# A fused attention and mixer kernel: the second-pass flag made behind the last output products, one output product in halves, 20 instead of 16 products of zeros at the begin, one transposition later

## The chip, the cores and the metric

The kernel runs on 1 core of one Trainium2 chip. A core has a matrix engine (TensorE, PE in the profile, with its weight loads as a row of their own, PEld), three engines for work on vectors (VectorE, DVE; ScalarE, ACT; GpSimd, POOL), and SyncE (SP), which here only issues DMAs. Each engine takes its instructions in the order in which they were written and waits on semaphores for the others. A "q" behind a name (SPq, ACTq, PEldq) means the instruction queue of that engine: DMA issues, loads of a register and branches. The metric is the device time of one execution in microseconds (us); less is better.

## The reference

With x of 2048 tokens by 448 features, float32 throughout:

```
g = sigmoid((x * gate_w).sum(-1))
a = attention(x): 16 heads of 28, one shared k and v (x @ wk, x @ wv),
    softmax(q k^T / sqrt(28)) v, heads joined, @ wo
h  = gelu(layernorm(x) @ w1); each quarter of h shifted by +1, -1, +2, -2 tokens
x1 = x + shifted(h) @ w2
b  = x1 + gelu(layernorm(x1) @ w3) @ w4
out = g * a + (1 - g) * b
```

## The kernel before, in words

The operands of the projections are split into a high part (type `fp32r`) and the rest, and summed from three products, which is why one projection of 512 columns is eleven matmuls (`proj`, lines 134 to 140). The order of the instructions on each engine is the order of the program; no planner moves them.

**The begin.** Line 66 writes a tile of zeros (`warm`), and lines 96 to 98 multiply it 16 times with itself into a bank that nobody reads. PE then waits for the first chunk of `wqraw` (query weights, loaded by ACT's queue, line 292) and of `xkv` (the transposed input, SP's queue, line 293). `first_queries` (line 317 on) begins with eight matmul instructions straight on these float32 chunks (line 324) and goes on with 32 on the split chunks (line 328), which ACT (`wqh`, `ahk`) and DVE (`wql`, `alk`) make meanwhile. After it come `stage_q(4)` to `stage_q(11)`, each eleven matmuls into one bank, a copy by ACT (`qf`, line 316) and a DMA to memory (`qd`, line 317).

Between these stages stands the preparation of the mixer. `centre_w1` (lines 397 to 402) takes the mean out of `w1raw`: PE makes `wsum_ps` in the one bank called "misc", DVE reads it four times (line 401). `ln1_tile` takes the layernorm statistics of a token tile on DVE, and POOL makes 1/sigma of them (`rs_s`, line 149). `ln1_send(0)` transposes that on PE into the same bank "misc" (`rsT`, line 377), ACT copies it out (`rT`, line 379), SP stores it (`rsd`, line 381); `ln1_read(0)` reads it back spread over 112 partitions (`rsb`, line 386). SP issues in order, so the loads of the last quarter of x (`load_x(3)`, line 281; `load_x1(3)`, line 284) stand behind that read. `split_w_high` and `split_w_low` make `w1h` and `w1l` on ACT and DVE. `stage_w1(0)` needs `w1h`, `w1l`, and for its first DVE step (`hf`, line 453) `rsb`. `spare_h` and `spare_w2` move rows by DMA (lines 413 to 416 and 430 to 433) ahead of the products `hs` of `stage_w2` (line 471 on).

**The middle.** `stage_w1`, `stage_w2`, the MLP with w3 and w4, and then attention: 16 units (4 token blocks by 4 groups of 4 heads), 8 rounds each of scores (line 205), exponentials on ACT (line 872), values (line 883). The diff doesn't touch them.

**The end.** The last unit's sums over keys are made by lines 986 to 996: DVE puts the last parts together as `oo` (two halves of 256 tokens), PE adds up the denominators (`sums_to_queries`, line 1002), DVE takes reciprocals (`rr`, line 1009), PE spreads them over rows (line 1012), DVE multiplies (`on`, line 1016). Then `tail_wo` makes the last output products with `wo` (`wo_products`, line 831), adds on DVE (`ot`, line 847) and stores (line 1025). The group before the last (`u - 1`) still owes its product for token tile 3; line 994 puts it into bank 3, and `tail_wo(3, ...)` adds the last group's on top. `check` and the reduction into `worst` (line 1019) say whether any softmax denominator left its range; PE counts the good rows (`n_good`, line 1030), ACT turns the count into an integer (`redo`, line 1032), and every engine loads it (line 1036) and branches (line 1040) past a second pass that these inputs don't need.

Of the kernel before, what the change touches and what calls it, by code (L numbers as in the profile page):

```python
# [17 lines left out]
P = 128  # L18
# [19 lines left out]
def f32(ap):  # L38
    return ap.bitcast(F32)
# [3 lines left out]
def gated_mix_kernel(  # L43
# [12 lines left out]
    nc = tc.nc  # L56
# [33 lines left out]
    def misc_tile(name):  # L90
        return psA.tile([P, 512], F32, tag="misc", bufs=1, name=name)
# [2 lines left out]
        return psA.tile([P, 512], F32, tag="mx", bufs=1, name=name)  # L94

    wps = misc_tile("warm_ps")
    for _ in range(16):
        nc.tensor.matmul(wps[:, 0:256], warm[:, 0:P], warm, start=True, stop=True)

    def split_w_chunk(raw, wh, wl, c, cols=slice(None)):  # L100
# [9 lines left out]
    def split_w_high(raw, wh, wl):  # L110
        nc.scalar.copy(wh[:, 0:3, :], raw[:, 0:3, :])
        nc.gpsimd.memset(f32(wh)[64:128, 3, :], 0.0)
        nc.scalar.copy(wh[0:64, 3, :], raw[0:64, 3, :])
        nc.scalar.copy(wl[64:128, 3, :], raw[64:128, 3, :])

    def split_w_low(raw, wh, wl):
        for c in range(3):
            nc.vector.tensor_tensor(wl[:, c, :], raw[:, c, :], f32(wh)[:, c, :], ALU.subtract)
        nc.vector.tensor_tensor(wl[0:64, 3, :], raw[0:64, 3, :], f32(wh)[0:64, 3, :], ALU.subtract)
# [14 lines left out]
    def proj(ps, wh, wl, ah, al):  # L134
        for c in range(3):
            nc.tensor.matmul(ps, wh[:, c, :], ah[:, c, :], start=(c == 0), stop=False)  # L136
            nc.tensor.matmul(ps, wh[:, c, :], al[:, c, :], start=False, stop=False)  # L137
            nc.tensor.matmul(ps, wl[:, c, :], ah[:, c, :], start=False, stop=False)  # L138
        nc.tensor.matmul(ps, wh[:, 3, :], ah[:, 3, :], start=False, stop=False)  # L139
        nc.tensor.matmul(ps, wl[:, 3, :], ah[:, 3, :], start=False, stop=True)  # L140

    def stats_tile(pool, b, t, mv):
        st = pool.tile([P, 6], F32, tag="st", bufs=4, name=f"st_{pool.name}_{b}_{t}")
        nc.vector.bn_stats(st, x1[:, 4 * b + t, :])
        nc.vector.bn_aggr(mv[:, t, :], st)
# [5 lines left out]
    def stats_tiles(pool, b):  # L151
        return (pool.tile([P, 4, 2], F32, tag="mv", bufs=2, name=f"mv_{pool.name}_{b}"),
                pool.tile([P, 4], F32, tag="rs", bufs=2, name=f"rs_{pool.name}_{b}"))
# [106 lines left out]
    with tc.tile_pool(name="s1b", bufs=1) as s1b, \  # L260
# [34 lines left out]
        w1h = s1.tile([P, 4, D], F32R, name="w1h")  # L295
        w1l = s1.tile([P, 4, D], F32R, name="w1l")
# [16 lines left out]
        def q_out(u, ps):  # L313
            b, g = divmod(u, NG)
            qf = s1.tile([P, 512], F32, tag="qf", bufs=4, name=f"qf_{u}")
            nc.scalar.copy(qf, ps)
            nc.scalar.dma_start(qd[g, :, 512 * b:512 * b + 512], qf)
# [13 lines left out]
        def stage_q(u, tile_of=mm1):  # L331
            b, g = divmod(u, NG)
            ps = tile_of(f"q_{u}")
            w = slice(g * P, (g + 1) * P)
            proj(ps, wqh[:, :, w], wql[:, :, w], *xact[b])
            q_out(u, ps)
# [31 lines left out]
        def ln1_tile(b, t):  # L368
            if t == 0:
                rs1_of[b] = stats_tiles(s1, b)  # L370
            stats_tile(s1, b, t, rs1_of[b][0])
            if t == 3:
                stats_end(*rs1_of[b])

        def ln1_send(b):
            ps = misc_tile(f"rsT_{b}")[0:4, 0:P]
            nc.tensor.transpose(ps, rs1_of.pop(b)[1], ident)
            rT = s1.tile([4, P], F32, tag="rT", bufs=2, name=f"rT_{b}")
            nc.scalar.copy(rT, ps)
            rb_of[b] = dram.tile([4, P], F32, tag="rsd", bufs=2, name=f"rsd_{b}")  # L380
            nc.sync.dma_start(rb_of[b], rT)
# [99 lines left out]
        w1raw = f32(s1b.tile([P, 4, 516], F32R, tag="hl", bufs=2, name="w1raw"))[:, :, 0:D]  # L481
# [28 lines left out]
        centre_w1()  # L510
        stage_q(7)
        stage_q(8)
        ln1_send(0)
        ln1_read(0)
        split_w_high(w1raw, w1h, w1l)
        for t in range(4):
            ln1_tile(1, t)
        split_w_low(w1raw, w1h, w1l)
        stage_q(9)
        load_x(3)  # L520
        stage_q(10)
        load_x1(3)
# [233 lines left out]
    with tc.tile_pool(name="s3", bufs=1, reuse_waits="tile") as s3, \  # L756
# [77 lines left out]
        ot_of = {}  # L834
        whole = slice(0, D)
        halves = [slice(0, D // 2), slice(D // 2, D)]

        def wo_products(u, t, ps, cols=whole, start=True, stop=True):
            by_columns(ps, on_of[u], t, wof[:, u % NG, cols], start, stop)
# [73 lines left out]
        for c in range(NC):  # L913
            u, i = divmod(c, NT // 2)
# [62 lines left out]
        u = NU - 1  # L977
# [6 lines left out]
        wo_banks = [singles[0], singles[1], singles[2], singles[3], pairs[0][:, 1]]  # L984

        for k in (2 * NC - 2, 2 * NC - 1):
            for i in range(2):
                for j in range(4):
                    nc.tensor.matmul(pv[i][32 * j:32 * j + 32, :], vext[:, k % NT, :], p_of[k][:, j, sides[i]],
                                     start=(k % 2 == 0), stop=(k % 2 == 1), tile_position=(0, 32 * j))  # L990
            if k % 2 == 0:
                run_jobs(singles[1], 1)
        assert [job[2] for job in jobs] == [(u - 1, 3), (u - 1, 3)]
        wo_products(u - 1, 3, wo_banks[3][:, whole], stop=False)
        for i in range(2):
            nc.vector.tensor_add(o[:, sides[i]], part[:, sides[i]], pv[i])
        sums = [singles[1][:, 0:8], pairs[1][:, 0, 0:8]]
# [10 lines left out]
        for i in range(2):  # L1008
            nc.vector.reciprocal(rr[:, 8 * i:8 * i + 8], sums[i])
            for t in (2 * i, 2 * i + 1):  # L1010
                for j in range(4):
                    nc.tensor.matmul(rows[i][32 * j:32 * j + 32, t % 2 * P:t % 2 * P + P],
                                     rr[:, 4 * t + j:4 * t + j + 1].broadcast_to([P, 32]), ident,
                                     start=True, stop=True, tile_position=(0, 32 * j))
        for i in range(2):
            nc.vector.tensor_mul(on[:, sides[i]], o[:, sides[i]], rows[i])
        check(rr.rearrange("p (a b) -> p a b", b=4), 4)
# [1 line left out]
        nc.vector.tensor_reduce(worst, good, axis=AX.XY, op=ALU.min)  # L1019
        n0 = NT - 4  # L1020

        def tail_wo(t, ps, cols, queue, start=True):
            wo_products(u, t, ps, cols, start=start)
            wo_add(u, t, ps, cols)
            queue.dma_start(out[0, (n0 + t) * P:(n0 + t + 1) * P, cols], ot_of[n0 + t][:, cols])

        tail_wo(0, wo_banks[0][:, whole], whole, nc.sync)
        tail_wo(1, wo_banks[1][:, whole], whole, nc.scalar)
        n_good = pairs[1][0:1, 0, 0:1]
        nc.tensor.matmul(n_good, worst, ones, start=True, stop=True)  # L1030
        redo = s3.tile([1, 1], mybir.dt.int32, name="redo")
        nc.scalar.activation(redo, n_good, AF.Copy, bias=float(P), scale=-1.0)
        tail_wo(3, wo_banks[3][:, whole], whole, nc.sync, start=False)
        tail_wo(2, wo_banks[2][:, halves[0]], halves[0], nc.scalar)
        tail_wo(2, wo_banks[4][:, halves[1]], halves[1], nc.scalar)
        again = nc.values_load(redo, min_val=0, max_val=P,
                               skip_runtime_bounds_check_because="it is P less a count of at most P flags of 0 or 1")

# [1 line left out]
        with tc.If(again > 0, label="redo"):  # L1040
            for b in range(NB):
                for g in range(NG):
                    u = b * NG + g
# [6 lines left out]
                    for kt in range(NT):  # L1050
                        ps = [bank(f"s2_{u}_{kt}_{j}") for j in range(4)]
# [4 lines left out]
                        for j in range(4):  # L1056
                            nc.tensor.matmul(pv[32 * j:32 * j + 32, :], vext[:, kt, :], p[:, j],
                                             start=(kt == 0), stop=(kt == NT - 1), tile_position=(0, 32 * j))
# [3 lines left out]
                    for t in range(4):  # L1062
                        ps = bank(f"wo2_{u}_{t}")[:, whole]
# [55 lines left out]
```

## Time and profile before

| what | us |
|---|---|
| median of 3 runs (lowest, highest) | 928.12 (927.07, 928.72) |
| the profiled execution, its own time | 929.3 |
| its span, first to last instruction | 927.4 |
| PE busy, share of the span | 913.3 (98%) |
| ACT busy | 636.0 (69%) |
| DVE busy | 519.3 (56%) |

In the rows that follow, a row of the timeline is start, duration, engine, line, operation, output<-inputs, form, count, and in brackets the idle time ahead of it and what ended it. A row of the chain of waits is start, duration, engine, tile and line: the chain runs from the last instruction back, at each step to what released it, and so says which work sets the end. The groups merge instructions that follow each other closely, so that their pieces overlap in print. PEclk in a table of stretches is the share of TensorE's clock that was granted; the record of it begins with the first change of the clock, and what lies ahead of that is printed as 1.00.

### The profile page before, as it was taken

The numbers are of one execution on the slowest core, as the hardware profiler recorded it, in microseconds if no ns is written. First come the engines' busy times: TensorE is split into PE (matmuls) and PEld (weight loads), VectorE is DVE, ScalarE is ACT, GpSimd is POOL, SyncE is SP. The second block draws the span as 40 slices with busy tenths as digits, with TensorE's granted clock in tenths as the row PEclk, the third lists the DMA queues.
The fourth block names the chain that finished last, engine by engine and source line by source line (L and its number), as shares of the span: only waits on it lengthen the run. The fifth ranks groups of instructions, "written<-read, shape, count | busy, mean of one in ns | idle before, by whom it ended". The sixth has DMA issues, their size and how long they took to land.

```text
span 927.4 us, 24251 instructions
## 1 busy us (share of the span) xinstructions
PE 913.3 (98%) x10348; PEld 627.8 (68%) x10348; DVE 519.3 (56%) x965; ACT 636.0 (69%) x1002; POOL 80.3 (9%) x116
## 2 busy tenths in 40 slices
PE   9999999999999999999999999999999999999997
PEld 6788888888888888875555555555555555555553
DVE  3665273631431431146666776777667767766664
ACT  5542345322222132169999999999999999999994
POOL 3243320200000520020000000000000000000000
PEclk9999999999999999999999999999999999999999
DMA  9822643120110110010000001000011000010001
GB/s 309 296 66 55 183 131 126 39 66 1 40 46 2 33 53 1 1 51 23 17 22 21 16 20 49 23 25 15 25 33 39 20 24 14 25 44 13 14 14 43
DMA packets 40584, 47.32 MB, mean 51 GB/s; under 512 B 10137, under 2 KB 28633, under 8 KB 40473
## 3 DMA queue, kind: packets, MB, share of 16 engines
q1 hardware_dynamic: 37160, 40.04, 14.7%
q10 hardware_dynamic: 3312, 5.70, 1.7%
q8 instruction: 82, 1.34, 0.6%
q14 instruction: 30, 0.24, 0.1%
HBM read 32.56 MB, written 11.67 MB: 48 GB/s over the span
## 4 chain that ended last, share of the span: by engine, by line
PE 94%; ACT 4%; issue 1%; DVE 1%; DMA 1%; DVEq 0%; ACTq 0%
PE bank L883 25%; PE bank L205 18%; PE bank L831 5%; PE acc L693 5%; PE acc L695 5%; PE acc L694 5%; PE g L137 4%; PE g L138 4%; PE g L136 4%; ACT p L872 4%; PE pair L205 2%; PE hs L471 1%; PE hs L472 1%; PE g L140 1%; PE g L139 1%; PE h L136 1%
## 5 line engine op out<-in xcount | busy, mean ns | idle before, releaser
L872 ACT ACTIVATE p<-bank 128x512 f32<-128x512 f32 x512 | 265.5, 611 | 11.1 <-POOL ones L857 4.2
L883 PE MATMUL bank<-p,vext 128*32 128x256 f32 x4064 | 248.4, 382 | 5.7 <-ACT p L872 2.0
L883 PEld LDWEIGHTS bank<-p,vext 128*32 128x32 f32 x4064 | 119.0, 109 | 124.4 <-ACT p L872 59.8
L929 DVE COPY p<-pair 128x1024 f32<-128x1024 f32 x127 | 155.6, 1225 | 54.9 <-PE pair L205 40.1
L683 ACT ACTIVATE gh<-g 128x512 fp32r<-128x512 f32 x55 | 32.9, 599 | 187.3 <-PE g L140 187.3
L805 DVE TENSOR_TENSOR o<-o,bank 128x256 f32<-128x256 f32 x222 | 93.5, 421 | 90.1 <-PE bank L883 73.9
L872 ACT ACTIVATE p<-p 128x1024 f32<-128x1024 f32 x127 | 139.8, 1101 | 0.0
L872 ACT ACTIVATE p<-pair 128x1024 f32<-128x1024 f32 x129 | 137.3, 1064 | 0.0
L685 DVE TENSOR_TENSOR gl<-gf,gh 128x512 fp32r<-128x512 f32 x55 | 38.2, 694 | 168.6 <-ACT gf L684 168.6
L205 PE MATMUL bank<-qh,kh 32*128 32x512 f32 x512 | 116.4, 448 | 0.1
L205 PE MATMUL pair<-qh,kh 32*128 32x512 f32 x512 | 116.1, 449 | 0.3 <-DVE x L750 0.3
L205 PE MATMUL bank<-qh,kl 32*128 32x512 f32 x512 | 102.1, 390 | 0.0
L205 PE MATMUL pair<-qh,kl 32*128 32x512 f32 x512 | 101.5, 390 | 0.0
L205 PE MATMUL bank<-ql,kh 32*128 32x512 f32 x512 | 101.3, 388 | 0.0
L205 PE MATMUL pair<-ql,kh 32*128 32x512 f32 x512 | 100.7, 388 | 0.0
L205 PEld LDWEIGHTS bank<-qh,kh 32*128 32x128 f32 x512 | 48.1, 181 | 60.7 <-issue 34.3
L693 PE MATMUL acc<-w4h,gh 128*128 128x448 f32 x220 | 80.6, 366 | 0.0
L695 PE MATMUL acc<-w4h,gl 128*128 128x448 f32 x220 | 80.4, 366 | 0.0
L694 PE MATMUL acc<-w4l,gh 128*128 128x448 f32 x220 | 80.2, 364 | 0.0
L137 PE MATMUL g<-al,w3h 128*128 128x512 f32 x168 | 65.9, 393 | 0.0
L138 PE MATMUL g<-ah,w3l 128*128 128x512 f32 x168 | 65.9, 392 | 0.0
L136 PE MATMUL g<-ah,w3h 128*128 128x512 f32 x168 | 65.8, 392 | 0.0
(210 smaller groups left out, 1402.1 us busy)
## 6 DMA issues: line engine op xcount, KB each, us to landing
qd<-qf ACTq DMA_DIRECT2D x16, 256.0 KB
rb<-rd SPq DMA_DIRECT2D x15, 256.0 KB
x<-in_x_dram SPq DMA_DIRECT2D x4, 896.0 KB
xd<-xt SPq DMA_DIRECT2D x16, 224.0 KB
w34raw<-in_w_dram SPq DMA_DIRECT2D x7, 512.0 KB
qr<-qd SPq DMA_DIRECT2D x64, 56.0 KB
w34raw<-in_w_dram SPq DMA_DIRECT2D x7, 448.0 KB
out_dram<-ot SPq DMA_DIRECT2D x14, 224.0 KB
```

The costliest lines, as they stand in the source:

```text
L136: nc.tensor.matmul(ps, wh[:, c, :], ah[:, c, :], start=(c == 0), stop=False)
L137: nc.tensor.matmul(ps, wh[:, c, :], al[:, c, :], start=False, stop=False)
L138: nc.tensor.matmul(ps, wl[:, c, :], ah[:, c, :], start=False, stop=False)
L205: nc.tensor.matmul(ps[j], k[h, keys], q[h, :], start=(r == 0), stop=(r == 2), tile_position=(32 * j, 0))
L693: nc.tensor.matmul(ps, gh[:, tok], w4h[i][:, k, :], start=(f == 0), stop=False)
L694: nc.tensor.matmul(ps, gh[:, tok], w4l[i][:, k, :], start=False, stop=False)
L695: nc.tensor.matmul(ps, gl[:, tok], w4h[i][:, k, :], start=False, stop=(f == stop))
L805: nc.vector.tensor_add(o, o, pv)
L831: nc.tensor.matmul(ps[32 * i:32 * i + 32, :], a[:, c:c + 32], w, start=start, stop=stop, tile_position=(0, 32 * i))
L872: nc.scalar.activation(p[:, heads], p[:, heads] if source is None else source, AF.Exp, scale=SCALE)
L883: nc.tensor.matmul(pv[32 * j:32 * j + 32, :], vext[:, kt, :], p_of[k][:, j, qs], start=(k == ks[0]), stop=(k == ks[-1]), tile_position=(0, ...
L929: nc.vector.tensor_copy(pa[:, both], pairs[0])
```

## The change

Four edits. The begin has 20 products of zeros in place of 16. The transposition of the first block's 1/sigma, with the copy, the store and the read that follow from it (`ln1_send(0)`, `ln1_read(0)`), stands behind `stage_q(9)` and behind the splits of `w1`; with it `split_w_low` moves ahead of `ln1_tile(1, t)`. At the end the product that the group `u - 1` owes is made in two halves of 224 columns, the second one behind the spreading of the reciprocals. And the flag (`n_good`, `redo`) is made behind the last output product, with the two half stores of tile 2 issued by ACT behind it.

```
     wps = misc_tile("warm_ps")
-    for _ in range(16):
+    for _ in range(20):
         nc.tensor.matmul(wps[:, 0:256], warm[:, 0:P], warm, start=True, stop=True)
...
         stage_q(8)
+        split_w_high(w1raw, w1h, w1l)
+        split_w_low(w1raw, w1h, w1l)
+        for t in range(4):
+            ln1_tile(1, t)
+        stage_q(9)
         ln1_send(0)
         ln1_read(0)
-        split_w_high(w1raw, w1h, w1l)
-        for t in range(4):
-            ln1_tile(1, t)
-        split_w_low(w1raw, w1h, w1l)
-        stage_q(9)
         load_x(3)
...
-        wo_products(u - 1, 3, wo_banks[3][:, whole], stop=False)
+        wo_products(u - 1, 3, wo_banks[3][:, halves[0]], halves[0], stop=False)
...
+        wo_products(u - 1, 3, wo_banks[3][:, halves[1]], halves[1], start=False, stop=False)
         for i in range(2):
             nc.vector.tensor_mul(on[:, sides[i]], o[:, sides[i]], rows[i])
...
-        def tail_wo(t, ps, cols, queue, start=True):
+        def tail_store(t, cols, queue):
+            queue.dma_start(out[0, (n0 + t) * P:(n0 + t + 1) * P, cols], ot_of[n0 + t][:, cols])
+
+        def tail_wo(t, ps, cols, start=True):
             wo_products(u, t, ps, cols, start=start)
             wo_add(u, t, ps, cols)
-            queue.dma_start(out[0, (n0 + t) * P:(n0 + t + 1) * P, cols], ot_of[n0 + t][:, cols])
-
-        tail_wo(0, wo_banks[0][:, whole], whole, nc.sync)
-        tail_wo(1, wo_banks[1][:, whole], whole, nc.scalar)
+        tail_wo(0, wo_banks[0][:, whole], whole)
+        tail_store(0, whole, nc.sync)
+        tail_wo(1, wo_banks[1][:, whole], whole)
+        tail_store(1, whole, nc.scalar)
+        tail_wo(3, wo_banks[3][:, whole], whole, start=False)
+        tail_store(3, whole, nc.sync)
+        tail_wo(2, wo_banks[2][:, halves[0]], halves[0])
+        tail_wo(2, wo_banks[4][:, halves[1]], halves[1])
         n_good = pairs[1][0:1, 0, 0:1]
         nc.tensor.matmul(n_good, worst, ones, start=True, stop=True)
         redo = s3.tile([1, 1], mybir.dt.int32, name="redo")
         nc.scalar.activation(redo, n_good, AF.Copy, bias=float(P), scale=-1.0)
-        tail_wo(3, wo_banks[3][:, whole], whole, nc.sync, start=False)
-        tail_wo(2, wo_banks[2][:, halves[0]], halves[0], nc.scalar)
-        tail_wo(2, wo_banks[4][:, halves[1]], halves[1], nc.scalar)
+        for cols in halves:
+            tail_store(2, cols, nc.scalar)
```

The first place is ACT's row at the begin, where the copy `rT` of the transposed 1/sigma stands among the copies `qf` of the query stages (`qd` is their DMA) and the high parts `w1h` of the weights. Before:

```order
L316 COPY qf_332<-q_320 128x512
L317 DMA qd<-qf_332 128x512
L379 COPY rT_337<-rsT_335 4x128
L111 CAST w1h<-w1raw 128x1344
L113 CAST w1h<-w1raw 64x448
L114 CAST w1l<-w1raw 64x448
L316 COPY qf_379<-q_367 128x512
```

Now:

```order
L316 COPY qf_336<-q_324 128x512
L317 DMA qd<-qf_336 128x512
L111 CAST w1h<-w1raw 128x1344
L113 CAST w1h<-w1raw 64x448
L114 CAST w1l<-w1raw 64x448
L316 COPY qf_375<-q_363 128x512
L317 DMA qd<-qf_375 128x512
L379 COPY rT_380<-rsT_378 4x128
```

`rT` moved behind the three casts and behind the copy and the DMA of the ninth query stage; on PE the transposition `rsT` moved in the same way behind the eleven matmuls of that stage, and the rows of SP and POOL kept their order.

The second place is PE's row at the end, from the denominators (`oo` with `pick`) to the load of the flag; `on_11206` and `on_11210` are the last group's rows, `on_10944` those of the group before it, and `worst` is what the flag is counted from. Before:

```order
L1002 MATMUL pair_3240<-pick,oo_11205 128x4 x2
L1012 MATMUL bank_3237<-ident,rr_11234 32x128 x8
L1012 MATMUL pair_3240<-ident,rr_11234 32x128 x8
L831 MATMUL bank_3235<-wof,on_11206 32x448 x4
L831 MATMUL bank_3236<-wof,on_11206 32x448 x4
L1030 MATMUL pair_3240<-ones,worst 1x1
L831 MATMUL bank_3238<-wof,on_11206 32x448 x4
L831 MATMUL bank_3237<-wof,on_11206 32x224 x4
L831 MATMUL pair_3239<-wof,on_11206 32x224 x4
L1036 TENSOR_LOAD redo
```

Now:

```order
L1002 MATMUL pair_3244<-pick,oo_11209 128x4 x2
L1012 MATMUL bank_3241<-ident,rr_11238 32x128 x8
L1012 MATMUL pair_3244<-ident,rr_11238 32x128 x8
L831 MATMUL bank_3242<-wof,on_10944 32x224 x4
L831 MATMUL bank_3239<-wof,on_11210 32x448 x4
L831 MATMUL bank_3240<-wof,on_11210 32x448 x4
L831 MATMUL bank_3242<-wof,on_11210 32x448 x4
L831 MATMUL bank_3241<-wof,on_11210 32x224 x4
L831 MATMUL pair_3243<-wof,on_11210 32x224 x4
L1039 MATMUL pair_3244<-ones,worst 1x1
L1044 TENSOR_LOAD redo
```

A half of the owed product now stands between the spreading of the reciprocals and the last group's products, and the count of the flag moved from behind the second of these to the very end.

## The prediction

> **What bounds the kernel now.** First the page: who carries the chain of waits.
>
> ```profile
> span 927.4 us, 24251 instructions
> PE 94%; ACT 4%; issue 1%; DVE 1%; DMA 1%; DVEq 0%; ACTq 0%
> ```
>
> TensorE sets the end. The list of what PE waited for over the whole span is short; these come first, and the two rows behind them name DVE:
>
> ```profile
> PE bank L883 <- ACT p L872: 2.0, 7, 0.3
> PE warm_ps L98 <- DVE warm L66: 1.0, 1, 1.0
> PE q L324 <- DMA wqraw<-in_wq_dram: 0.8, 1, 0.8
> ```
>
> The only transfer among them is the first load. After it PE never waits for one, so time taken out of PE's begin should move everything behind it, unless something that is hidden today comes late.
>
> Next the begin: the timeline of PE and of its weight loads, and one row of the chain of waits.
>
> ```profile
> 1.05 3.59 PE L98 MATMUL warm_ps<-warm 128*128 128x256 bf16 x16 [1.05 <-DVE warm L66]
> 5.42 5.86 PE L324 MATMUL q<-xkv,wqraw 128*128 128x512 f32 x8 [0.77 <-DMA wqraw<-in_wq_dram]
> 8.99 0.33 PEld L324 LDWEIGHTS q<-xkv,wqraw 128*128 128x128 f32 x1 [0.52 <-issue]
> 9.83 0.19 PEld L324 LDWEIGHTS q<-xkv,wqraw 128*128 128x128 f32 x1 [0.50 <-issue]
> 10.26 0.19 PEld L324 LDWEIGHTS q<-xkv,wqraw 128*128 128x128 f32 x1 [0.24 <-issue]
> ```
>
> ```profile
> 11.28 7.27 PE q L328 x32
> ```
>
> The same weight load takes 0.33 us at 8.99 and 0.19 from 9.83 on, and the loads follow each other after 0.84 us (9.83 less 8.99), then after 0.43 (10.26 less 9.83). So TensorE's clock doubles at about 9.8. The 3.59 us of zeros did not raise it, and PE then stood idle for 0.77 us; real products raised it 4.4 us after 5.42. From L328 on a product takes 7.27/32 = 0.23.
>
> Last the end of the chain:
>
> ```profile
> 914.09 0.38 PE bank L831 x8
> 915.33 0.75 PE bank L831 x8
> 917.71 0.43 DVE on L1016
> 918.19 2.56 PE bank L831 x19
> ```
>
> At 915.33 the owed product (448 columns, 0.75) stands on the path ahead of the denominators; at 914.09 one of 224 columns takes 0.38.
>
> **The change part by part.** *20 products of zeros.* One takes 3.59/16 = 0.224 us, so 20 end at 1.05 + 4.49 = 5.54, and the hole of 0.77 us closes. Their own price lies between 0 (the hole takes them) and 5.54 - 5.42 = 0.12; I take 0.1. Their worth depends on when the clock rises. If it takes unbroken work, then more than the 3.59 us that weren't enough and at most the 4.4 that were: counted from 1.05 it rises by 5.45, when the first real product starts. The eight L324 products then run at 0.43 throughout. The slow stretch was 9.83 - 5.42 = 4.41 us, half of it lost: 2.2 us. Bounds: 2.2, and 0 if work on zeros doesn't count. I take 2.2, because the row of the 16 zeros is only 0.8 us short of the real products' 4.4; less 0.1, the begin gives 2.1.
>
> What follows must be ready 2.1 us sooner. L328 now starts when L324 ends, 11.28; DVE has its first chunk long before, and the last chunk of weights, for `stage_q(4)`, is ready at 12.26, 6 us ahead of that stage (11.28 + 7.27 = 18.55):
>
> ```profile
> 6.97 0.69 DVE L130 TENSOR_TENSOR alk<-xkv,ahk 128x512 fp32r<-128x512 f32 x1 [5.98 <-ACT ahk L127]
> 11.57 0.69 DVE L103 TENSOR_TENSOR wql<-wqraw,wqh 128x512 fp32r<-128x512 f32 x1 [0.40 <-ACT wqh L102]
> ```
>
> So the 2.1 us pass through.
>
> [...]
>
> *The transposition later.* Left where it is, it would meet these rows:
>
> ```profile
> 29.07 2.21 DVE L401 SCALAR_TENSOR_TENSOR w1raw<-wsum_ps,w1raw 128x448 f32<-128x448 f32 x4
> 31.65 0.27 PE L377 MATMUL rsT<-ident,rs_s 128*4 128x128 f32 x1
> 33.47 0.34 SPq L381 DMA_DIRECT2D rsd<-rT  x1
> 35.16 0.57 ACT L114 CAST w1l<-w1raw 64x448 fp32r<-64x448 f32 x1
> 35.34 0.33 SPq L386 DMA_DIRECT2D rsb<-rsd  x1
> 35.77 0.55 SPq L281 DMA_DIRECT2D xkv<-in_xT_dram  x1
> 42.01 0.69 DVE L453 TENSOR_TENSOR hf<-h,rsb 112x512 f32<-112x512 f32 x1 [0.32 <-PE h L140]
> 52.41 0.69 DVE L453 TENSOR_TENSOR hf<-h,rsb 112x512 f32<-112x512 f32 x1 [0.41 <-DMA rsb<-rsd]
> ```
>
> `rsT` needs the bank that DVE reads until 31.28. At 31.65 it just fits; 2.1 sooner it would hold PE for up to 1.7 us. Behind `stage_q(9)`, eleven products of 0.23 = 2.5 us, it comes at 32.0 and waits for nobody, even if DVE has moved by nothing. What it pushes: `rT` now stands behind the three casts, which end at 35.73, and behind a `qf`; `rsd` is issued near 36.5, the read `rsb` 1.87 later (as 35.34 less 33.47), near 38.4, and `load_x(3)` and `load_x1(3)`, queued behind it on SP, near 38.8: 3 us later. The read that was issued at 35.34 was there for DVE at 42.01, 6.7 us on; DVE now wants it at 39.9, 1.5 us after its issue. So `hf` may come some us late against PE. DVE then has one `hf` (0.69) and one split of that size per group of eleven products (2.5), so it gains 1.1 us a group, and the banks of `h` turn over in fours: PE would feel it after four groups. `w1l` now stands ahead of the statistics on DVE and is ready no later. Counted at nothing; without that cover it is the third rival. POOL's queue is unchanged.
>
> *The half product.*
>
> ```profile
> 914.98 0.42 DVE L996 TENSOR_TENSOR oo<-o,pair 128x256 f32<-128x256 f32 x1
> 917.46 0.62 PE L1012 MATMUL pair<-ident,rr 128*32 128x128 f32 x16
> 920.88 0.57 PE L831 MATMUL pair<-wof,on 128*32 128x224 f32 x8
> ```
>
> It takes 0.75 - 0.38 = 0.37 us from ahead of the denominators; `oo`'s first half is there at 915.40, so they start 0.37 earlier, and so does `on`: ready at 917.77, not 918.14. The other 0.38 follow PE's spreading products, whose last row then ends at 918.08 - 0.37 = 917.71. The timeline prints 0.57 for eight products of 224 columns where the chain has 0.38, so some 0.19 of a row's end is overlapped by what follows: the half runs from about 917.52 to 917.90, and the last group's products start some 0.04 behind it, at 917.94, and not at 918.19. Gain 0.25, between 0.1 (nothing overlaps) and 0.37.
>
> *The flag.*
>
> ```profile
> 919.72 0.17 PE L1030 MATMUL pair<-ones,worst 128*1 128x1 f32 x1
> 921.08 0.16 ACT L1032 ACTIVATE redo<-pair 1x1 int32<-1x1 f32 x1 [6.92 <-PE bank L831]
> 921.85 0.85 ACTq L1025 DMA_DIRECT2D out_dram<-ot  x2
> L1040 SPq EVENT_SEMAPHORE  x8: 17/17/17, 923.0 to 926.0; - x8
> ```
>
> `n_good` leaves the middle of the last products; it overlaps those around it: 0.03 gained, between 0 and 0.17. `redo` must now wait for the last product, 921.45 - 0.28 = 921.17, then 0.17 and 0.16 for itself: 921.5. The half stores queued behind it on ACT wait for DVE's `ot` until 921.85 - 0.28 = 921.57 anyway, so they lose nothing, by 0.07 us; a later flag costs what it is later. The other engines load the flag some 0.2 us later than now, and ACT, whose load stands behind its stores, still branches last. Sum at the end: 0.28.
>
> Together 2.1 + 0 + 0.28 = 2.4 us: the span 927.4 becomes 925.0, the execution's own 929.3 becomes 926.9. The median of the runs shown lies 1.2 us below that profiled execution; 928.12 - 2.4 = 925.7.
>
> **The rivals.** [...]
>
> *Zeros don't count.* No row shows zeros raising the clock. Then the end alone gains: 928.12 - 0.28 = 927.8.
>
> *Slower: the loads pushed back on SP.* `load_x(3)` and the next `rsd` and `rsb` (the DVE row at 52.41 already waited 0.41 for it) run into each other, and the rows that `stage_w2` needs come late:
>
> ```profile
> 54.43 0.59 SPq L433 DMA_DIRECT2D hl<-hl  x1
> 59.74 0.36 PE L471 MATMUL hs<-w2h,hh 128*128 128x448 f32 x1
> ```
>
> Issued at 54.43 and landed, by the 1.87 of `rsd`, at about 56.3, they have 3.4 us now and 1.3 with PE 2.1 us sooner. Past 57.6 PE waits; past 60.0 the whole gain is gone, past 61.9 the kernel is slower by 0.2%: 930.0. That takes a slip of 5.6 us, from loads that start 3 us later. A smaller slip that gives back half of the begin ends at 926.8.
>
> *The last store's tail goes.* SP waits 2.1 us in one piece near the end, while hardly anything moves:
>
> ```profile
> SPq L1040 <- SPq L1040: 3.2, 4, 2.1
> 924.00:924.50 0.50, 0.00 (x0) 0.00 (x0) 0.00 (x0) 0.00 (x0) 0.00 (x0) 1.00 0.00 0
> 925.00:925.50 0.50, 0.00 (x0) 0.00 (x0) 0.00 (x0) 0.00 (x0) 0.00 (x0) 0.50 0.06 9
> q8 instruction: 1, 0.02, 3.2%
> ```
>
> No bytes at 924.0, a trickle until 925.5: some packets of the last store come 1.5 us after the rest. The last row, of the stretch 923.5 to 926, is one code fetch: 3.2% of 16 engines x 2.5 us = 1.3 us of one DMA engine, time enough to hold them up. With the stores 0.28 sooner and PE's branch 0.2 later the fetch may miss them: 925.7 - 1.5 = 924.2, if the timed runs have that tail at all.
>
> **How the numbers follow.** Chances: forecast (925.7) 0.32, fixed stretches (926.1) 0.2, the tail gone too (924.2) 0.2, zeros don't count (927.8) 0.13, half given back (926.8) 0.1, slower (930.0) 0.05. The range goes from 924.2 to 927.8 with 0.2 on each side, since the middle of three runs that spread over 1.65 is no firmer: 924.0 to 928.0. About 0.2% (1.9 us, so 926.3) is what a measurement can tell from no change. Faster: most of the first (0.28), six tenths of the second (0.12) and all of the third, 0.6; slower 0.06; the rest 0.34. The likeliest alone: 925.2 to 926.3.
>
> **What would show it.** Right: no idle PE ahead of L324, weight loads of 0.19 there by 6.4 or earlier, L328 2 us sooner, no transfer among PE's waits behind the first load, `on` 0.37 and the last `ot` 0.28 sooner as counted from the end of the values. Wrong: weight loads of 0.33 up to 9; PE waiting at L377, for a bank of `h` or at L471; the last two stores more than 0.1 us behind their `ot`; SP's last wait longer than 2.1.

## The result, and the profile after

| what | before | after |
|---|---|---|
| median (lowest to highest), 10 runs each, us | 928.63 (927.07 to 931.87) | 925.5 (924.77 to 926.98) |
| ratio, 95% interval | | 0.9964 (0.9954 to 0.9974) |
| the profiled execution, its own time and span, us | 929.3, 927.4 | 925.3, 923.5 |

By the ratio the change makes the kernel 3.3 us faster (2.4 to 4.3); the medians lie 3.1 apart; 925.7 was forecast. The two profiled executions differ by more, 4.0 us of span. The page of the changed kernel, its shares of the chain of waits, and then what PE waited for in the whole span:

```profile
span 923.5 us, 24276 instructions
PE 95%; ACT 3%; issue 1%; DVE 1%; DMA 0%; ACTq 0%
```

```profile
PE bank L883 <- ACT p L872: 2.0, 7, 0.3
PE warm_ps L98 <- DVE warm L66: 1.1, 1, 1.1
PE q L324 <- DMA wqraw<-in_wq_dram: 0.4, 1, 0.4
```

PE's only transfer is still the first load. It stands on the chain in both profiles, with 4.64 us before and 4.58 after, which prints as 1% and as 0%. Now the begin: the timeline of PE and its weight loads in the changed kernel, and two rows of its chain.

```profile
1.05 3.88 PE L98 MATMUL warm_ps<-warm 128*128 128x256 bf16 x20 [1.05 <-DVE warm L66]
5.36 3.70 PE L324 MATMUL q<-xkv,wqraw 128*128 128x512 f32 x8 [0.43 <-DMA wqraw<-in_wq_dram]
5.89 0.19 PEld L324 LDWEIGHTS q<-xkv,wqraw 128*128 128x128 f32 x1 [0.24 <-issue]
```

```profile
5.36 3.70 PE q L324 x8
9.06 7.30 PE q L328 x32
```

Twenty zeros took 3.88 us and not 3.59 x 20/16 = 4.49: the last of them already ran at the doubled clock, which the trace's record has up from 4.21 on. The weight loads of L324 take 0.19 from 5.89 on, and L328 stands on the chain at 9.06, where it stood at 11.28: 2.2 us sooner. (In the timeline, whose rows overlap, it starts at 8.49 and started at 10.71; the times of L328 below are of that kind.) PE still had a hole of 0.43 us ahead of L324, since faster zeros end sooner; the clock was not lost by it.

The end, first on the chain, then the last rows of DVE, ACT and their queues in the timeline:

```profile
913.26 0.38 PE bank L831 x8
913.64 0.54 PE bank L1002 x4
915.20 0.44 PE pair L1012 x16
915.64 2.68 PE bank L831 x32
918.34 1.40 DVE ot L847 x3
```

```profile
915.27 0.42 DVE L1017 TENSOR_TENSOR on<-oo,bank 128x256 f32<-128x256 f32 x1 [0.33 <-PE bank L1012]
919.14 0.16 ACT L1041 ACTIVATE redo<-pair 1x1 int32<-1x1 f32 x1 [7.04 <-PE pair L1039]
919.30 0.44 DVE L847 SCALAR_TENSOR_TENSOR ot<-pair,gg,ot 128x224 f32<-128x224 f32 x1
919.42 0.85 ACTq L1024 DMA_DIRECT2D out_dram<-ot  x2
```

The last `ot` of the kernel before was this row:

```profile
921.73 0.44 DVE L847 SCALAR_TENSOR_TENSOR ot<-pair,gg,ot 128x224 f32<-128x224 f32 x1
```

The owed product is 0.38 instead of 0.75. From it to the last `ot` before: 921.73 - 915.33 = 6.40 us; after: 919.30 - 913.26 = 6.04. So the two edits of the end give 0.36 on PE and DVE. The count is done when the last `ot` starts (919.14 and 0.16), and the half stores are issued as soon as `ot` allows.

What follows the last issue shrank by far more. SP's last wait, and the line on which SP waits for the stores and the engines branch:

```profile
SPq L1048 <- SPq L1048: 1.7, 4, 0.6
```

```profile
L1048 SPq EVENT_SEMAPHORE  x8: 17/17/17, 920.6 to 922.1; - x8
L1048 PEldq COMPARE_BRANCH  x1: 410/410/410, 920.0 to 920.0; - x1
```

Before, SP waited 2.1 us in its last piece and its row ended at 926.0; the last two stores were issued from 921.85 on. From that issue to SP's last event are 926.0 - 921.85 = 4.15 us before, and 922.1 - 919.42 = 2.7 after. This 1.5 us is the largest surprise.

The difference of the two spans, 4.0, is thus: 2.1 from the begin (what is left of its 2.2 where the owed product starts, 915.33 less 913.26), 0.36 from the end's products, 1.5 from the last store.

### The profile page after: what moved, and what is told of

The parts are those of the page before. It is cut to its first block, busy times and chain, and to the rows that moved or that the text cites. A ratio compares the mean times of both kernels' runs of the same rounds, so it can differ in the third digit from the quotient of the medians.

```text
span 923.5 us, 24276 instructions
## 1 busy us (share of the span) xinstructions
PE 911.5 (99%) x10360; PEld 627.6 (68%) x10360; DVE 519.2 (56%) x965; ACT 635.2 (69%) x1002; POOL 79.4 (9%) x116
## 4 chain that ended last, share of the span: by engine, by line
PE 95%; ACT 3%; issue 1%; DVE 1%; DMA 0%; ACTq 0%
PE bank L883 26%; PE bank L205 18%; PE bank L831 5%; PE acc L693 5%; PE acc L695 5%; PE acc L694 5%; PE g L137 4%; PE g L138 4%; PE g L136 4%; ACT p L872 3%; PE pair L205 3%; PE hs L471 1%; PE hs L472 1%; PE g L140 1%; PE g L139 1%; PE h L136 1%
## 5 line engine op out<-in xcount | busy, mean ns | idle before, releaser
L883 PE MATMUL bank<-p,vext 128*32 128x256 f32 x4064 | 248.4, 382 | 5.7 <-ACT p L872 2.0
L883 PEld LDWEIGHTS bank<-p,vext 128*32 128x32 f32 x4064 | 119.1, 109 | 124.4 <-ACT p L872 59.9
```

## The experiments

Twelve runs, two of them of unaltered kernels. Each was timed beside the kernel before; medians are in us, changes are the ratio less one. "Half", "late flag", "move" and "20 zeros" name the four edits. They ran on three chips, four to a chip in the order of the table; the kernel before had a median of 929.25 (35 runs), 929.25 (35 runs) and 928.72 (33 runs) there.

| kernel | median | change, 95% interval |
|---|---|---|
| 20 zeros alone | 927.82 | -0.11% (-0.20 to -0.02) |
| 20 zeros and move | 927.43 | -0.15% (-0.24 to -0.06) |
| half and late flag | 927.27 | -0.22% (-0.31 to -0.14) |
| move alone | 929.33 | +0.05% (-0.04 to +0.13) |
| late flag alone | 927.70 | -0.17% (-0.26 to -0.08) |
| half alone | 929.04 | -0.06% (-0.16 to +0.05) |
| the kernel before, unaltered | 928.78 | -0.05% (-0.15 to +0.04) |
| changed kernel, 28 zeros | 926.97 | -0.21% (-0.30 to -0.12) |
| changed kernel, 0 zeros | 927.30 | -0.10% (-0.19 to -0.01) |
| before, branch later | 927.20 | -0.18% (-0.28 to -0.08) |
| changed kernel without the move | 925.88 | -0.27% (-0.40 to -0.14) |
| the changed kernel, unaltered | 926.17 | -0.27% (-0.36 to -0.18) |

The begin's two edits (0.15%) and the end's two (0.22%) add up to 0.37%, which is the whole change (0.36% and 0.27% in two measurements).

### The begin alone: 20 zeros, then with the move

```
-    for _ in range(16):
+    for _ in range(20):
```

> The kernel before with 20 products of zeros and nothing else. If the closed hole is what lets the clock rise early, the weight loads of L324 take 0.19 us by 6.4 at the latest, in every profile. If the moved transposition is needed to keep that gain, PE waits at L377 for DVE's last read of the bank (0.5 to 1.7 us) and the time falls by only 0.5 to 1.5 us. If it isn't needed (DVE moves along with PE), PE waits nowhere and the time falls by 1.7 to 2.2 us. If zeros don't count: no change, weight loads of 0.33 up to 9.

With the transposition moved as well (`split_w_low`, then `stage_q(9)`, then `ln1_send(0)` and `ln1_read(0)`):

> 20 products of zeros and the transposition moved, the end as before. Theory: 1.7 to 2.2 us less than before, PE waits nowhere at L377, SP's last wait is about 2 us as before, because the end is untouched. Rival, the begin gives little and the measured gain came from the end: less than 0.7 us.

Measured: 0.11% and 0.15%, that is 1.0 and 1.4 us, where the sum had 2.1. The medians lie 1.4 and 1.8 us below that of the kernel before, and the intervals (0.2 to 1.9 and 0.6 to 2.2) reach to about the sum. 1.7 to 2.2 was expected where PE doesn't wait at L377. It waits there in neither profile, L328 starts at 8.63 and 8.66, and the last store still has its long tail (SP's last wait is 2.0). So the zeros do raise the clock, but by the ratios they bring only half to two thirds of what one profile shows.

### The end alone

The half product, the stores behind the products, and the flag behind both, with 16 zeros and the transposition where it was.

> The half product and the late flag, the begin as before (16 products of zeros). Theory, the last store's tail belongs to the runs of the kernel before and goes with the late flag: 1 to 1.9 us less, SP's last wait about 0.6 us. Rival, the tail was an accident of one profile: 0.3 to 0.4 us less, which can hardly be told from nothing.

Measured: 2.0 us (1.3 to 2.9), where the sum had 0.28. SP's last wait is 0.5 here. The tail of the last store is the reason, as the next runs show.

### The move alone

```
-        ln1_send(0)
-        ln1_read(0)
         split_w_high(w1raw, w1h, w1l)
+        split_w_low(w1raw, w1h, w1l)
         for t in range(4):
             ln1_tile(1, t)
-        split_w_low(w1raw, w1h, w1l)
         stage_q(9)
+        ln1_send(0)
+        ln1_read(0)
```

> The transposition moved alone, 16 products of zeros, the end as before. Theory: no change within 0.3 us, as PE did not wait for it and nothing that it pushes back is waited for by PE. Rival, the loads pushed back on SP reach PE: slower by 0.5 us or more with a new row among PE's waits between 40 and 75.

Measured: no change. This is the term that stood at nothing.

### The flag alone, the half product alone, and the kernel before once more

The late flag alone; the last lines in their order after the edit, with the one that is new marked:

```
         tail_wo(2, wo_banks[2][:, halves[0]], halves[0])
         tail_wo(2, wo_banks[4][:, halves[1]], halves[1])
         n_good = pairs[1][0:1, 0, 0:1]
         nc.tensor.matmul(n_good, worst, ones, start=True, stop=True)
...
+        for cols in halves:
+            tail_store(2, cols, nc.scalar)
```

> The kernel before with the late flag alone (made behind the last output product, the two half stores of tile 2 behind it). Theory: the branch comes later against the last store, so that the code fetch misses it: SP's last wait 0.6 us instead of 2.1, and 1 to 1.5 us less. Rival, the flag does nothing but leave PE's row: 0 to 0.2 us less.

The half product alone:

```
-        wo_products(u - 1, 3, wo_banks[3][:, whole], stop=False)
+        wo_products(u - 1, 3, wo_banks[3][:, halves[0]], halves[0], stop=False)
...
+        wo_products(u - 1, 3, wo_banks[3][:, halves[1]], halves[1], start=False, stop=False)
```

> The kernel before with the owed product in halves alone. Theory: the denominators 0.37 us sooner, the last output products 0.25 to 0.3 us sooner, and the same tail at the last store: 0.3 us less at most. Rival, the 0.3 us alone get the stores out of the code fetch's way: 1.5 us less.

The kernel before once more. A "stretch" here is a step of the clock's own record: the traces have the clock up for 914.77 us before and for 918.19 in the changed kernel, which differ by 3.41, and a "look" is the end of such a step.

> The kernel before, unchanged, for a second profile. Theory: the clock rises between 8.8 and 12.3 us, at a time that has nothing to do with the first profile's 9.8, unless a look falls where the 3.6 us of zeros fill a stretch alone (about one execution in ten); SP's last wait is near 2.1 again if the tail belongs to the program, and near 0.6 if it was an accident. The time agrees with that of the kernel before within 0.3 us.

The flag alone gives 0.17% (1.6 us); its own work on PE was worth 0.03. The half product's 0.06% cannot be told from nothing, which agrees with the 0.3 us that were expected. SP's last wait with the late flag alone, and then with the half product alone:

```profile
SPq L1047 <- SPq L1047: 1.6, 4, 0.5
```

```profile
SPq L1041 <- SPq L1041: 3.3, 4, 2.2
```

The long piece of 2.0 to 2.2 us follows the place of the flag: it stands in all six profiles of kernels that make and read the flag in the middle, and in none of the seven with the late flag (0.5 to 0.6 there).

The profile of the half product alone shows two other things. Its clock rose early, although it has 16 zeros; and then PE waited where the transposition stands:

```profile
30.23 2.20 DVE L401 SCALAR_TENSOR_TENSOR w1raw<-wsum_ps,w1raw 128x448 f32<-128x448 f32 x4
32.58 0.27 PE L377 MATMUL rsT<-ident,rs_s 128*4 128x128 f32 x1 [2.23 <-DVE w1raw L401]
```

So 16 zeros sometimes suffice, and oftener than the one execution in ten that was expected. Of the profiles with 16 zeros, four have the early rise (the move, the flag, the half product, and the unaltered kernel before) and three have it at 9.7 to 9.9 (the first profile of before, the end alone, the later branch). The unaltered kernel before showed it in its times too: six of its twelve runs lie from 927.05 to 928.37, six from 929.18 to 929.95, and nothing between. Of the 103 runs of the kernel before beside the experiments about a third lie below 928.65, but there the two groups run into each other. That the lower group is the executions with the early rise is what the profiles suggest; a run without a profile does not show its clock.

### The later branch: is it the code fetch?

The kernel before, with every product and store in its place; only the engines read the flag later.

```
         tail_wo(2, wo_banks[4][:, halves[1]], halves[1], nc.scalar)
+        redo_late = s3.tile([1, 1], mybir.dt.int32, name="redo_late")
+        nc.scalar.copy(redo_late, redo)
-        again = nc.values_load(redo, ...
+        again = nc.values_load(redo_late, ...
```

> The kernel before, with one addition: the flag is counted in the middle of the last products as before, but ACT copies it once more behind the issue of its last two stores, and the engines load that copy, so that every branch comes later (about 922.9 in the frame of before, behind the issue of the last store at 922.3) while all products and stores keep their places. Theory of the code fetch (PE branches while the last store's packets are still to be queued, its fetch on one DMA engine then holds back some of them): with the branch later by 1.5 us or more the fetch comes behind the packets; last store's issue to last landing falls from 3.7 to about 2.1, and the median is 1.5 us below the kernel before less what the later branch itself costs (0 to 0.5): -1.0 to -1.5. Rival (it is the place of the counting product, or the order of stores and counting on ACT, that matters): the interval stays 3.6 to 3.8 and the median is the same or up to 0.5 us slower.

Measured: 0.18% faster (1.7 us; 0.7 to 2.6). ACT's stores in the timeline, the rows of the branch, and SP's last wait:

```profile
922.39 0.85 ACTq L1025 DMA_DIRECT2D out_dram<-ot  x2
```

```profile
L1042 SPq EVENT_SEMAPHORE  x8: 17/17/17, 924.8 to 925.4; - x8
L1042 PEldq COMPARE_BRANCH  x1: 504/504/504, 924.4 to 924.4; - x1
```

```profile
SPq L1042 <- SPq L1042: 0.5, 1, 0.5
```

The stores and products are those of the kernel before, and PE branches at 924.4 in place of 922.1. SP's short wait alone would not show a quicker store, since SP too branches later. The packets of the two half stores show it: from the issue at 922.39 to the end of the last packet, 924.36, are 1.97 us; in the kernel before, from 921.85 to 925.46, they are 3.61. So it is not the place of the counting product nor ACT's order that held the last store up, but when the engines branch. To SP's last event the gain is smaller, 3.0 us in place of 4.15, as the late branch costs some 0.5 of its own; the 1.7 us of the medians agree with that within their interval.

The code fetch itself stands in the list of DMA queues as q8. The stretch is 924.6 to 927 us here:

```profile
q8 instruction: 1, 0.02, 2.8%
```

2.8% of 16 engines x 2.4 us is 1.1 us of one DMA engine, and it lies behind the stores. In the kernel before the fetch fell into 923.5 to 926, among the packets of the last store. In the changed kernel one stands in 921 to 922.6:

```profile
q8 instruction: 1, 0.02, 4.2%
```

What the DMA engines moved in those two stretches, before and then in the changed kernel; each number is a fortieth of the stretch, and a packet's bytes are counted where it starts:

```profile
GB/s 578 315 230 101 160 0 131 0 0 0 0 0 0 0 0 0 131 0 0 0 14 0 14 14 0 14 14 0 14 14 14 0 0 0 0 0 0 0 0 0
```

```profile
GB/s 381 358 358 336 381 247 157 272 45 23 205 410 0 0 0 0 0 0 0 0 0 0 0 0 0 0 0 205 0 0 0 0 0 0 0 0 0 0 0 0
```

14 GB/s in 0.0625 us is one packet of 896 bytes, that is one row of the half store. Before, the fetch is one packet of 16 KB that starts at 923.54 and ends at 924.83. By 923.85 all of the store's packets are done but nine: eight of 896 bytes and a last one of 4. They follow one after another from 924.79 to 925.46. The half store is 128 packets of 896 bytes and 16 of 4, so these nine, eight and one, are a sixteenth of it: the share of one of the 16 engines and, by the times, of the one that was fetching. The same nine begin within 0.04 us of the end of the fetch in all six kernels that read the flag early. In the changed kernel the order is the other one: the last packet of the store ends at 921.45, and there the fetch starts (the 410 in the second row).

The fetch follows the branch: it starts 1.40 us behind PE's branch before (923.54 less 922.14) and 1.40 in the changed kernel (921.45 less 920.05), and 1.3 to 1.6 us behind it in thirteen of the fourteen profiles (1.96 in the other). Neither it nor the nine packets are broken up by the other.

How narrow it is: PE branches at 922.14 before, and the second of ACT's two stores is issued at 922.29; after, the branch is at 920.05 and that issue at 919.86. The rows, before and after:

```profile
L1040 PEldq COMPARE_BRANCH  x1: 504/504/504, 922.1 to 922.1; - x1
L1025 ACTq DMA_DIRECT2D out_dram<-ot x3: 344/353/416, 920.7 to 922.3; - x3
```

```profile
L1024 ACTq DMA_DIRECT2D out_dram<-ot x3: 344/353/409, 918.3 to 919.9; - x3
```

Some 0.34 us between the two decide over 1.5. In other profiles the bound is closer still: with the move alone PE branches 0.05 us ahead of that issue, and the tail is there; with the flag and the half product late (the end alone) it branches 0.07 behind, and the tail is gone.

### The changed kernel with 28 zeros and with none

```
-    for _ in range(20):
+    for _ in range(28):
```

> The changed kernel with 28 products of zeros. Theory of fixed stretches: with the clock up by 4.5 to 7.9 in either case, 8 more products cost 0.1 us each when the clock is up and 0.2 when not, 0.4 to 1.4 us later at the first real product: 0.3 to 1.3 us slower than with 20. Rival, the clock needs more unbroken work than 20 products give: as fast as with 20, or faster.

The zeros now stand on the chain, which with 20 of them begins with the first load:

```profile
1.05 4.70 PE warm_ps L98 x28
5.75 3.47 PE q L324 x8
```

They put L328 off by 0.1 to 0.2 us (it starts at 8.66; 8.49 and 8.54 in the two profiles of the changed kernel), and with the clock already up before L324 (its eight products take 3.63 us, 3.70 with 20 zeros, 5.86 before) there is nothing that they could bring. The median is 926.97; the changed kernel itself has 925.5 and 926.17 in its two measurements, on other occasions and the second on another chip. Against the kernel before beside it the change is -0.21%, and -0.36% and -0.27% for the unaltered changed kernel, with intervals that overlap. So no gain over 20 is seen; that 28 cost 0.3 us or more, as expected, is not shown.

```
-    for _ in range(20):
+    for _ in range(0):
```

In a stretch of 3.41 us, 2.70 us of busy PE did not raise the clock (the end alone) and 2.74 did (the half product alone); that is what "about eight tenths" stands on.

> The changed kernel with no products of zeros: PE stands idle until the first load lands at about 5.4 us. Theory of stretches (the clock rises at the end of the first stretch of 3.41 us of which about eight tenths were busy; stretches fall anywhere): the first such stretch begins at the latest 0.7 us after 5.4 and ends between 8.1 and 11.5, so the clock rises there in every execution, on the mean about 9.8, and no execution has the early rise. Against the changed kernel with 20 zeros (rise 3.8 to 5.2, slow work lost 0) the eight L324 products take 2.0 to 2.9 us longer: a median 2.2 us above the changed kernel's own, with one narrow hump rather than two, and a profile with weight loads of 0.33 at 8 us. Rival (what matters is the work in total, zeros counting as a head start that is lost for good): the same sign, but the clock rises 4.4 us after 5.4, at 9.8, always. Rival (zeros don't count, and the begin's gain of the change came from elsewhere): the median equals that of the changed kernel within 0.3 us.

PE waited 5.4 us for the first load, and the weight loads got faster late, as expected:

```profile
8.09 0.34 PEld L324 LDWEIGHTS q<-xkv,wqraw 128*128 128x128 f32 x1 [0.52 <-issue]
8.94 0.26 PEld L324 LDWEIGHTS q<-xkv,wqraw 128*128 128x128 f32 x1 [0.52 <-issue]
9.44 0.19 PEld L324 LDWEIGHTS q<-xkv,wqraw 128*128 128x128 f32 x1 [0.24 <-issue]
```

But the median is only 1.1 us above that of the unaltered changed kernel on the same chip (927.30 and 926.17; by the ratios to the kernel before it is 1.6), not 2.2: a miss by up to half. The profiles say where part of it went. L328 starts 1.8 us later without zeros (10.33 and 8.54), `hs` at L471 only 1.4 later (59.38 and 57.99), the last values only 0.7 (L989 at 912.19 and 911.49). The first 0.4 is a wait of PE's weight loads in this profile of the unaltered changed kernel, at 18.5 us, which the kernel without zeros doesn't have:

```profile
PEld q L139 <- DVE ahk L132: 0.5, 1, 0.5
```

The tokens for the query stages came late by that much for the early PE. The first profile of the changed kernel has no such wait, so it is not there in each execution. The other 0.7 arises in the 500 us of attention, whose length differs between profiles by up to 1.4 us (502.1 to 503.5 from the first L883 to the first L989) without any relation to the edits that could be found. Whether the begin's gain is regularly lost there in part, or this was chance, stays open.

### Without the move

The changed kernel with `ln1_send(0)` and `ln1_read(0)` back ahead of the splits; and the changed kernel once more as the measure.

> The changed kernel without the move: 20 zeros, the half product and the late flag, the transposition back ahead of the splits. Theory (the move is an insurance): where the loads of the mixer's weights and of x let DVE finish L401 by 29.5, nothing is lost; where L401 ends at 31.7, PE waits up to 2.2 us at L377. So the median is 0 to 1 us above the changed kernel's own on this chip, and a profile shows PE waiting at L377 only if L401 starts at 29 or later. Rival (the move costs by pushing SP's loads back): the median is 0.3 us or more below the changed kernel's.

> The changed kernel once more, unaltered, beside the three others on the same chip: 925.5 to 926.5, 0.25 to 0.4% below the kernel before. It gives the measure for the three others, and for the 28 zeros, which came out 1.5 us above it on another chip.

The medians are equal (925.88 and 926.17). What PE waited for without the move:

```profile
PE rsT L377 <- DVE w1raw L401: 0.9, 1, 0.9
```

And two of the eleven runs without the move took 928.34 and 929.80, while none of the eleven with it passed 926.94. Two runs are few, but they have the size of the wait at L377 with the half product alone (2.2 us there). So the move looks like an insurance; the times do not show that it pays. DVE's L401 starts anywhere from 27.0 to 30.2 us in the profiles with an early clock (in the latest, DVE had waited for ACT's `ahk`, whose chunk of `xkv` landed at 22.95), and PE waits at L377 for the late ones. PE was expected to wait only where L401 starts at 29 or later; in the profile without the move L401 starts at 28.25. With the transposition behind `stage_q(9)` PE waited there in none of six profiles. The insurance has its price in margin, in the timeline of the changed kernel and in DVE's waits from 30 to 60 us:

```profile
37.46 0.26 ACT L379 COPY rT<-rsT 4x128 f32<-4x128 f32 x1 [0.40 <-PE q L140]
39.63 0.33 SPq L386 DMA_DIRECT2D rsb<-rsd  x1
55.17 0.59 SPq L433 DMA_DIRECT2D hl<-hl  x1
```

```profile
DVE hf L453 <- DMA rsb<-rsd: 7.1, 2, 4.0
```

DVE waited 7.1 us for `rsb` (0.4 before), and the last rows for `stage_w2` are issued at 55.17, 2.4 us ahead of the first `hs` at 57.56 (5.3 before). By the 1.9 us that `rsd` takes from issue to landing (39.63 less 37.74), an estimate for these rows, 0.5 us are left. But L433 fills `hl`, which the products at L474 read, from 58.38 on; L471 reads `hh`, whose last rows are issued at 53.90. By the same estimate 1.3 and 1.8 us are left. PE did not wait.

## Why the prediction was right, and where it was not

**The time.** 925.7 was forecast and 925.5 came out, but that they lie so near is luck. The forecast took 2.4 us off a median of 928.12, and the change took off 3.3. The begin was taken for too much (2.1; 1.4 by the ratio), the end for far too little (0.28; 2.0), and the median before is 928.63 over ten runs.

**20 products of zeros: direction right, the worth mis-sized on the mean.** The step was "its worth depends on when the clock rises", with 2.2 lost and 0.1 paid. In the profile it is 2.2. In the times it is 1.0 to 1.4 (20 zeros alone, and with the move), though their intervals are wide. The step that failed is taking the one profiled execution of before for all: there the clock rose at 9.8, but with 16 zeros it rises early in about a third to a half of the executions, and those had nothing to gain. The spread of the three runs, 1.65 us, was in the prediction, as a reason for a wider range; it should also have scaled the forecast's own term. The own price of the zeros was 0 in the profile, not 0.1: the faster zeros end before the load lands. And "the 2.1 us pass through" was argued from the weights alone: in the second profile of the changed kernel the stage behind L328 waits 0.5 us for tokens (`ahk`).

**The rival of fixed stretches was right on the mechanism.** The clock falls behind the kernel before, and then behind the changed kernel, at these places (stretches of 0.01 us; PEclk is the third column from the end):

```profile
924.56:924.57 0.01, 0.00 (x0) 0.00 (x0) 0.00 (x0) 0.00 (x0) 0.00 (x0) 1.00 0.00 0
924.57:924.58 0.01, 0.00 (x0) 0.00 (x0) 0.00 (x0) 0.00 (x0) 0.00 (x0) 0.50 0.00 0
```

```profile
922.39:922.40 0.01, 0.00 (x0) 0.00 (x0) 0.00 (x0) 0.00 (x0) 0.00 (x0) 0.85 0.00 0
922.40:922.41 0.01, 0.00 (x0) 0.00 (x0) 0.00 (x0) 0.00 (x0) 0.00 (x0) 0.50 0.00 0
```

In the traces' record of the clock it is up from 9.80 to 924.57 before and from 4.21 to 922.40 in the changed kernel, and it stays up for 914.77, 918.19 or 921.60 us in all fourteen profiles. These differ by 3.413, and are 268, 269 and 270 times 3.4133. So the clock changes on a grid of that step. In the changed kernel it was up for 269 of them, from 1.1 us before L324 on, which agrees with the 3.88 us of the zeros. Neither 5.45 (unbroken work) nor 6.39 (one step ahead of the 9.80 of before) was the time; stretches lie differently in each execution (the clock rose at 3.79, 3.82, 5.15 and 9.74 in four profiles with 16 zeros). The rival's 926.1 stands for a gain of 0.4 us less than the forecast's. No run shows that term: by the profile the full 2.2 came. "Zeros don't count" is refuted: the clock rose on nothing but zeros.

**The move: 0, right.** No product of PE waited for the rows that it pushed back, which is what the forecast counted on. But `rsd` was issued at 37.7, not 36.5, and of the 1.3 us that were to be left between L433's rows and L471 0.5 was left; the forecast was too sure there. It also set these rows against the wrong products: L433 fills `hl`, which L474 reads. The claim that a transposition left in place would hold PE up by as much as 1.7 us was right in kind: 0.2, 0.9 and 2.2 us were seen, and 0 in others, even with an early clock.

**The half product: right.** 0.37 us left the path ahead of the denominators as counted (0.75 and 0.38), and `on` came 915.27 - 913.26 = 2.01 us behind the owed product, 2.38 before. The gain to the last `ot` was 0.36 with the flag's part, where the sum had 0.28.

**The flag: the term of the sum was right, the tail was missed.** 0.03 us was its own work. Its worth was 1.5 to 1.7 us, by the code fetch that no longer comes ahead of one engine's share of the last store. This is the largest error of the sum, which held the flag's own work alone. The prediction had it as a rival with 0.2, by the right mechanism and the right size, and put the branch 0.2 us later than before as what might decide it. In fact the branch moved by 0.34 us against the last issue. Its doubt, "if the timed runs have that tail at all", is settled: the flag alone made the timed runs 1.6 us faster, the later branch alone 1.7. The chance of that rival was too low: the rows that it needed stood in the profile. `redo` was expected to end 0.07 us before DVE's `ot` let the stores go, and ended 0.12 before (919.30, and 919.42 for the issue), so ACT issued its half stores no later than `ot` allowed.

**Slower by loads pushed back on SP**, the third rival in the words on the transposition, and **half given back** by a smaller slip of the same rows did not come about: no product of PE waited for those rows in any profile. The 0.4 us that one profile of the changed kernel lost at 18.5 us is another wait, ahead of the moved transposition.

## What to carry to other kernels

Read the last microseconds behind the last issue as a stage of their own: a flag that is read early can make the engines fetch code while the last store is under way, and a later branch can be faster (here by 1.7 us). A warm-up should be long enough to fill a stretch of the clock wherever it begins (3.41 us here: 16 zeros brought the early rise in four of seven profiles, 20 zeros in five of five); one that suffices only in some executions can split the times into two groups, and a single profile then gives the gain of one group only. When the begin of a kernel is made faster, what stands on a fixed landing time (here L401 and its bank) can become the next wait (up to 2.2 us at L377). Moving work behind it took that wait out of the profiles; whether it pays was not shown by the medians.

## What the runs showed of the hardware

How busy a stretch of 3.41 us must be to raise the clock was seen sharply. The next rows are PE's busy time in the last stretch that did not raise the clock, in the kernel before and in the end alone (stretch, length, PE busy, count), and then in the stretch that did, with the half product alone and in the unaltered kernel before:

```profile
2.97:6.39 3.42, 2.65 (x9) 1.00 0.92 323
```

```profile
2.91:6.33 3.42, 2.70 (x10) 1.00 0.95 310
```

```profile
0.38:3.79 3.41, 2.74 (x13) 1.90 (x14) 0.17 (x1) 1.17 (x1) 2.98 (x11) 1.00 0.41 114
```

```profile
0.41:3.82 3.41, 2.77 (x14) 1.98 (x15) 0.17 (x1) 1.20 (x1) 2.99 (x10) 1.00 0.44 108
```

2.65 and 2.70 us of 3.41 did not raise it, 2.74 and 2.77 did: the bound lies near 0.79 to 0.80 of a stretch, by the profile's modelled ends of matmuls. Sixteen zeros are busy for 3.59 us and the hole behind them is 0.77 us, so whether a stretch fills depends on where it begins. An estimate from these rows: with a bound of 2.72 us, 16 zeros that run from 1.05 to 4.64 fill a stretch if it ends between 1.05 + 2.72 = 3.77 and 4.64 + 3.41 - 2.72 = 5.33. That is 1.56 of 3.41 us, or 46%; the four early rises lie from 3.79 to 5.15. Closing the hole then gains 2.2 us in the other 54%, 1.2 us on the mean, near the 1.0 to 1.4 measured. With 20 zeros all five profiles have the rise by 5.11.

And one packet of fetched code, 1.0 to 1.4 us on one DMA engine, can hold the end of a kernel up by 1.5 us.
